# First chunk of a chunked delta-rule kernel: block products without doubles, and weight loads held behind the second inverse

## The chip, the cores and the metric

The kernel runs on one core of a Trainium2 chip. The metric is the device time of one execution in microseconds; of several runs the median is given. A core has five engines that run their own instruction queues side by side and wait for each other through semaphores: PE (matrix products, with PEld for the loading of its stationary operand), DVE (vector), ACT (scalar and activation), POOL (GpSimd) and SP (here only a queue that issues DMA transfers). Matrix products land in PSUM, eight banks of 2 KB on each of 128 partitions; DVE and ACT bring them from there to SBUF.

## The reference

Two stages. The first is a delta rule over 768 tokens for 4 batches of 8 heads, each with a 48x48 state; the second is a feed-forward layer over the 3072 tokens of width 384 that come out.

```python
for t in range(S):                                  # q, k, v: (4, 8, 768, 48)
    kt, vt, bt = (k_n[:, :, t], v[:, :, t], beta[:, :, t, None])   # k_n: k over its norm
    y[:, :, t] = np.einsum('bhd,bhde->bhe', q[:, :, t], state)
    v_old = np.einsum('bhde,bhd->bhe', state, kt)
    state = state + bt[:, :, :, None] * np.einsum('bhd,bhe->bhde', kt, vt - v_old)
...
x = y.transpose(0, 2, 1, 3).reshape(3072, 384)
h = x @ w_in                                        # 384 x 2048, 64-bit in memory
g = np.maximum(h, 0.0) + alpha * np.minimum(h, 0.0)
return g @ w_out                                    # 2048 x 384, 64-bit in memory
```

## The kernel before

**Tiling.** The delta rule is done in 12 chunks of 64 tokens (`C = 64`). Inside a chunk the recurrence becomes a triangular system with one 64x64 matrix per head and batch. A step is one chunk of two of the four batches: `steps` has 24 of them, and steps 0 and 1 are the first chunk. A tile of a step has 128 partitions, 64 for each of its two batches, and 8 heads beside each other. `half(t)` is one batch's 64 partitions, `a` is a head's parity and `g` its number among the four of that parity (`G = 4`).

**The triangular system.** For the first four steps (`NJ = 4`) only diagonal blocks of 16x16 (`LB = 16`) are inverted, by elimination on DVE (`eliminate_small`), with everything turned so that a partition holds one matrix. The results are turned back in four pieces twice: first into `turned`, then into `inverse` (`back`, stream transposes at L567; `PIECES = 4`). `off_products` multiplies the block inverses with what lies off the diagonal (`mid`), which gives `diag` and, with the two halves of the partitions exchanged, `away`. Three substitutions with these (`substitute` L732 on PE, `substituted` L738 to L754 on DVE) then do what the remaining blocks ask for, `solve` (L910) multiplies with the inverses that `place_inverse` (L759) has laid out, and `outputs` (L923) makes the chunk's output, whose masked factor `a_t` comes from `mask` (L1623).

For odd heads (`a = 1`) substitutions 0 and 2 of steps 0 and 1 read `away`, and substitution 1 reads the upper half of the heads of `diag` with the halves exchanged in its output.

**What is a double here.** In `off_products`, for each of the two steps, PE makes the product of every head for both halves into its own half (L687: 16 matmuls); for the four odd heads it makes the same product once more into the other half (L689: 8 matmuls), so that `away` can be copied from PSUM. One ACT copy per step takes `diag` out (L690, 128x384) and one DVE copy takes `away` (L693, 128x192). Each float32 matmul shows as two records in the profile.

**Order of the work.** The schedule is manual: each engine does its instructions in the order in which the program issues them, and semaphores that follow from the data keep them correct. Generators (`inverted`, `conv_in`, `first_in`) are advanced by hand between other work. `weave` and `alongside` mix the first feed-forward products (L1088) with the second pair of steps (`second_pair`). PSUM is given out in turn: `ps_big` rotates three tiles of two banks, so a product waits until the tile's reader of three turns ago is done.

**Weights.** `w_in` and `w_out` have 64-bit elements. The `weights` helper loads each piece as raw words into a stage (512 KB for a piece of `w_in`), ACT does two passes over it (`begin`, L262 and L263), and DVE two more (`finish`, L272 and L277), after which the stage is free for a later piece. `w_in` has 12 pieces; six stages lie in the space of `w_out`, two in `space_out`. `fetch_in(n)` issues loads up to piece n, `begin_in(n)` ACT's passes, and `convert(n)` advances the generator `conv_in`, which itself calls `begin` for up to `ahead[0]` or one piece ahead. The first feed-forward products need pieces 0 to 2 for the first 512 columns, 3 to 5 for the next, and so on.

**Loads.** All loads but three of the first keys go through SP's queue, in order: first keys, beta, v and q of steps 0 and 1 (96 KB for each half), six weight pieces, two more once beta's place is free, keys of steps 4 to 6, the second copy of keys of step 1, v of 2, q of 2 and 3. A load that must wait for its place holds all that is behind it on SP.

**Filling PE.** `busy` issues wide matmuls whose results nobody reads, in the time in which DVE eliminates (L1606).

Of the kernel before, what the change touches and what calls it, by code (L numbers as in the profile page):

```python
# [25 lines left out]
FP32 = mybir.dt.float32  # L26
# [6 lines left out]
C = 64  # L33
HB = 32
# [10 lines left out]
def kernel(  # L45
# [623 lines left out]
    def off_products(both):  # L669

        x = [act[:, FP - 4 + i].rearrange("p f i -> p (f i)") for i in both]
        x = [y.rearrange("p (h c) -> p h c", h=H) for y in x]
        for i in both:
            own = turned[0][:, i * H : i * H + H]
            nc.scalar.mul(x[i][:, :, 0:HB], own, which[:, 0:1])
            nc.vector.tensor_scalar_mul(x[i][:, :, HB:C], own, which[:, 1:2])
        n = C - LB
        own, other = [ps_big(), None], ps_big()
        own[1] = ps_big()
        for i in both:  # L680
            p = own[i][:, 0, 0 : H * n].rearrange("p (b i) -> p b i", b=H)
            q = (other[:, 0] if i == 0 else own[1][:, 1])[:, 0 : G * n]
            q = q.rearrange("p (b i) -> p b i", b=G)
            for b in range(H):
                for t in range(2):
                    w, y = x[i][half(t), b], mid[i][half(t), b, LB:C]
                    nc.tensor.matmul(p[half(t), b], w, y)  # L687
                    if b >= G:
                        nc.tensor.matmul(q[half(1 - t), b - G], w, y)  # L689
            nc.scalar.copy(diag[i][:, :, LB:C], p)  # L690
            other_.append(q)
        return [
            lambda i=i: nc.vector.tensor_copy(out=away[i][:, :, LB:C], in_=other_[i])  # L693
            for i in both
        ]

    other_ = []
# [912 lines left out]

    def queries():
# [17 lines left out]

    def first_chunk(mask, inverted, convert):  # L1630
# [3 lines left out]
        aways = off_products(both)  # L1634
        for _ in range(PIECES - 1):
            next(inverted)
        aways[0]()
        next(inverted)
        assert next(inverted, None) is None
        aways[1]()  # L1640
        place_inverse(0)
# [3 lines left out]
        for k in range(3):  # L1645
            for i in both:
                p = substitute(i, now_at[i], k)
                if k == 0:
                    now_at[i] = work.tile([128, 2, G, D], FP32, name="r")
                substituted(i, now_at[i], p, k)  # L1650
                if i == 0 and k < 2:
                    now(flipped(NJ + k, ps_one()))
                if (k, i) == (1, 0):
                    place_inverse(1)
                if (k, i) == (0, 1):
                    place(0, (3,))
                    for j in (3, 2):
                        off_blocks(j, by_pool=True)
                if (k, i) == (1, 1):
                    place(1, (3,))  # L1660
                    begin_in(6)
                if i == 0 and k > 0:
                    mask(0, k - 1)
        for i in both:
            squared(NJ + i)
# [4 lines left out]
        now(weighted)  # L1670
        for a in range(2):
            mask(1, a)
        now(keys)
        now(solve(1))
# [3 lines left out]
        load_early(NJ + NKE)  # L1678
# [33 lines left out]
    n_in = FT * DM // n  # L1712
    stages = [space[:, i * n : (i + 1) * n] for i in range(n_in)]
    spare_words = space_out.rearrange("p s e -> p (s e)")
    stages += [spare_words[:, i * n : (i + 1) * n] for i in range(2)]
    ids = [*range(n_in + 2), 0, 2, 1, 3]
# [31 lines left out]
    fetch_in(n_in)  # L1748
# [61 lines left out]
    fetch_in(n_in + 2)  # L1810
# [9 lines left out]
    load_v(2)  # L1820
    for i in range(2):
        flips(N, i)
    for i in range(2):
        load_q(i + 2)
# [9 lines left out]
    busy(BUSY - 3.5, mid[1], p)  # L1834
    for _ in range(6):
        busy(0.25, mid[1], p)
    begin_in(5)
# [302 lines left out]
```

## Time and profile before

| what | value |
|---|---|
| median of 3 runs | 631.5 us (630.01, 631.5, 636.12) |
| profiled execution, its own time | 632.44 us |
| its span, first to last instruction | 630.7 us |
| PE busy in the span | 617.4 us (98%), 9116 matmul records |
| PEld busy | 545.5 us (86%) |
| DVE busy | 504.0 us (80%) |
| ACT busy | 312.4 us (50%) |
| POOL busy | 99.9 us (16%) |
| mean granted PE clock | 0.997 |
| DMA in the span | 39.26 MB, mean 62 GB/s; 17.98 MB of it in the first 100 us |

A line of the timeline names the start in us, the length, engine, line and operation, what it writes and reads, shapes, the number of instructions merged and, in brackets, the idle time before it with its cause; "issue" is a wait for which the profile shows no cause. Matmuls overlap and their ends are modelled. In the table of stretches each engine has its busy time in the stretch, and the last three columns are the granted PE clock, the share of the 16 DMA engines' time and the rate. The queue q8 carries instructions.

### The profile page before, as it was taken

What the parts mean: (1) busy time and instruction counts of PE and PEld (TensorE: products, weight loads), DVE (VectorE), ACT (ScalarE), POOL (GpSimd) and SP (SyncE); (2) the same over time, 40 slices, a digit from 0 to 9 for tenths busy, and PEclk for the clock granted to TensorE, in tenths of its full rate; (3) what the DMA queues carried; (4) which work ended last, traced back from release to release, by engine and by line L of the source; (5) the groups of instructions that cost most, each with busy time, mean ns of one, the idle gap of its engine ahead of it and who ended that gap; (6) DMA issues with size and microseconds to landing.
All of it is one profiled execution on the core that took longest, in us unless ns stands there. A gap on an engine that the chain in (4) does not pass through costs nothing.

```text
span 630.7 us, 21675 instructions
## 1 busy us (share of the span) xinstructions
PE 617.4 (98%) x9116; PEld 545.5 (86%) x9116; DVE 504.0 (80%) x1223; ACT 312.4 (50%) x836; POOL 99.9 (16%) x218
## 2 busy tenths in 40 slices
PE   6989999999999999999999999999999999999997
PEld 5678788566789989989989989989999999999997
DVE  5978999979989988968978868878979579386383
ACT  6878566255544256446345446335356366352230
POOL 7032221010001000000000000000053062061350
PEclk9989999999999999999999999999999999999999
DMA  7958845212252241241341121211220300100100
GB/s 117 301 120 193 242 87 161 41 38 51 44 85 44 56 73 27 54 74 30 51 76 30 39 40 27 53 26 27 46 51 13 62 15 11 30 3 1 26 1 25
DMA packets 145968, 39.26 MB, mean 62 GB/s; under 512 B 139040, under 2 KB 142256, under 8 KB 145872
## 3 DMA queue, kind: packets, MB, share of 16 engines
q1 hardware_dynamic: 144000, 37.40, 29.0%
q8 instruction: 71, 1.16, 0.7%
q10 hardware_dynamic: 1872, 0.49, 0.4%
q14 instruction: 25, 0.20, 0.1%
HBM read 33.14 MB, written 4.72 MB: 60 GB/s over the span
## 4 chain that ended last, share of the span: by engine, by line
PE 87%; DVE 5%; ACT 3%; DMA 2%; issue 1%; SPq 1%; ACTq 0%; DVEq 0%
PE p_ffn L1088 16%; PE p_ffn L1152 10%; PE p_more L1088 8%; PE p_more L1422 8%; PE p_more L1152 8%; PE p_ffn L1131 5%; PE p_more L1338 5%; PE p_ffn L1328 3%; PE p_ffn L1422 3%; PE p_ffn L1333 3%; PE p_pair L885 2%; PE p_pair L923 2%; PE p_pair L809 2%; PE p_pair L910 2%; PE p_pair L502 2%; PE p_pair L867 2%
## 5 line engine op out<-in xcount | busy, mean ns | idle before, releaser
L1088 PE MATMUL p_ffn<-xt,w_in 128*128 128x256 f32 x528 | 123.2, 384 | 0.1
L1088 PEld LDWEIGHTS p_ffn<-xt,w_in 128*128 128x128 f32 x528 | 97.6, 190 | 14.1 <-issue 0.4
L979 ACT COPY xt<-z 32x96 f32<-32x96 f32 x240 | 64.5, 269 | 49.4 <-DVE z L966 46.3
L1088 PE MATMUL p_more<-xt,w_in 128*128 128x256 f32 x240 | 55.7, 382 | 0.0
L1362 POOL TENSOR_TENSOR k_t<-k_t 128x128 f32<-128x128 f32 (+1 forms) x48 | 28.3, 591 | 166.3 <-ACT k_t L1357 163.8
L600 DVE TENSOR_TENSOR block<-block,prod 128x30 f32<-128x30 f32 (+9 forms) x150 | 50.0, 333 | 5.1
L1088 PEld LDWEIGHTS p_more<-xt,w_in 128*128 128x128 f32 x240 | 44.9, 190 | 6.3
L594 DVE TENSOR_TENSOR prod<-block 128x30 f32<-128x30 f32 (+9 forms) x150 | 48.6, 324 | 1.3
L419 POOL TENSOR_TENSOR beta_t<-beta_t,rec 128x8 f32<-128x8 f32 x24 | 6.9, 288 | 231.8 <-DVE rec L413 228.0
L1100 DVE SCALAR_TENSOR_TENSOR act<-act,al_t,p_ffn 128x256 f32<-128x256 f32 x72 | 31.0, 471 | 14.5 <-ACT act L1098 14.4
L826 ACT COPY inv<-p_pair 32x256 f32<-32x256 f32 x30 | 10.9, 363 | 59.2 <-DVE u L914 35.5
L1098 ACT ACTIVATE act<-p_ffn 128x512 f32<-128x512 f32 x36 | 21.4, 594 | 22.7 <-PE p_ffn L1088 22.4
L1362 POOL TENSOR_TENSOR block<-block 128x128 f32<-128x128 f32 (+1 forms) x48 | 27.7, 577 | 12.6 <-ACT block L1357 10.1
L1328 PE MATMUL p_ffn<-xt,w_in 128*128 128x256 f32 x96 | 29.3, 387 | 0.0
L1152 PE MATMUL p_ffn<-w_out,act 128*128 128x192 f32 x160 | 27.7, 327 | 0.0
L914 DVE TENSOR_TENSOR u<-p_pair,wgt 128x384 f32<-128x384 f32 x24 | 13.2, 554 | 16.8 <-PE p_pair L910 9.9
L1152 PEld LDWEIGHTS p_ffn<-w_out,act 128*128 128x128 f32 x160 | 26.2, 190 | 0.3
L1100 DVE SCALAR_TENSOR_TENSOR act<-act,al_t,p_more 128x256 f32<-128x256 f32 x40 | 17.3, 474 | 10.9 <-ACT act L1098 10.7
L895 DVE TENSOR_TENSOR r<-v_raw,p_pair 64x192 f32<-64x192 f32 (+1 forms) x66 | 23.2, 352 | 2.1 <-PE p_pair L885 1.0
L1152 PE MATMUL p_more<-w_out,act 128*128 128x192 f32 x128 | 22.3, 326 | 0.0
L1357 ACT COPY k_t<-p_more 128x512 f32<-128x512 f32 x16 | 9.4, 587 | 25.5 <-PE p_more L1338 18.9
L1422 PE MATMUL p_more<-w_out,act 128*128 128x192 f32 x128 | 21.6, 327 | 0.0
(285 smaller groups left out, 1486.5 us busy)
## 6 DMA issues: line engine op xcount, KB each, us to landing
w_out<-in_moe_w_in_dram SPq DMA_DIRECT2D x10, 512.0 KB, 5.6
v_raw<-in_v_dram SPq DMA_DIRECT2D x48, 96.0 KB, 2.9
kl<-in_k_dram SPq DMA_DIRECT2D x96, 48.0 KB, 2.4
out_dram<-o_sb SPq DMA_DIRECT2D x90, 48.0 KB, 1.6
space_out<-in_moe_w_out_dram SPq DMA_DIRECT2D x11, 384.0 KB, 4.0
ke_last<-in_k_dram SPq DMA_DIRECT2D x25, 96.0 KB, 3.5
qp<-in_q_dram SPq DMA_DIRECT2D x64, 32.0 KB, 2.2
w_out<-in_moe_w_out_dram SPq DMA_DIRECT2D x5, 384.0 KB, 5.3
```

Source lines behind the costliest of these rows:

```text
L594: nc.vector.tensor_tensor(out=prod, in0=r[:, 0:j, j : j + 1].to_broadcast([128, j, n]), in1=r[:, j : j + 1, j + 1 : HB].to_broadcast([128, ...
L600: nc.vector.tensor_tensor(out=r[:, 0:j, j + 1 : HB], in0=r[:, 0:j, j + 1 : HB], in1=prod, op=ALU.add)
L895: nc.vector.tensor_tensor(out=r[to, a], in0=v_in[to, a], in1=p[own, a, :, 0:D], op=ALU.subtract)
L979: nc.scalar.copy(to[quad(r), u, bp, t], z[quad(2 * t + u), r])
L1088: nc.tensor.matmul(p_h[:, i], w_in[:, t, (f + i) * 128 : (f + i + 1) * 128], xt[:, t], start=(t == 0), stop=(t == KT - 1),)
L1100: nc.vector.scalar_tensor_tensor(out=g[:, i], in0=g[:, i], scalar=al_t[:, f + i : f + i + 1], in1=p_h[:, i], op0=ALU.mult, op1=ALU.add,)
L1131: nc.tensor.matmul(p_o[u], gs[f // 2][:, f % 2, u * 128 : (u + 1) * 128], w_out[:, f], start=(f == 0), stop=(f == FT - 1),)
L1152: nc.tensor.matmul(p, x(i), w(i), start=(i == 0), stop=(i == FP - 1))
L1328: nc.tensor.matmul(p[:, f * 256 : f * 256 + 256], w(2, f), xt[:, 2], start=True, stop=False)
L1338: nc.tensor.matmul(q[:, j], a, b, start=True, stop=True)
L1362: nc.gpsimd.tensor_tensor(out=dst, in0=a, in1=b, op=ALU.add)
L1422: nc.tensor.matmul(p, x(i), w(i), start=(i == 0), stop=(i == FP - 1))
```

## The change

In `off_products` the second products of the odd heads are gone. Odd heads are multiplied once, into the exchanged half; ACT copies the even heads to `diag` and the odd ones to `away`, and POOL copies `away`, halves exchanged, to the upper heads of `diag`. DVE copies nothing there. `spread` is new and adds 16 matmuls of 32x32 on the four quarters, in a bank that nobody reads; `busy` has half a matmul less.

Four weight pieces are fetched ahead (`LOADED`) and four are converted by ACT before the first chunk. `release`, called when the second inverse is placed, writes one element of the fifth piece's stage from that inverse, so that this piece's load, and all that SP has behind it, waits for it; behind it come q of step 2, keys of step 7, pieces 5 to 7, v of 2 and q of 3. The squares of keys of steps 4 and 5 are made earlier, the last piece of the inverse is turned after the first substitution, and the four masks are moved.

```diff
@@ off_products
-        n = C - LB
-        own, other = [ps_big(), None], ps_big()
-        own[1] = ps_big()
         for i in both:
-            p = own[i][:, 0, 0 : H * n].rearrange("p (b i) -> p b i", b=H)
-            q = (other[:, 0] if i == 0 else own[1][:, 1])[:, 0 : G * n]
-            q = q.rearrange("p (b i) -> p b i", b=G)
-            for b in range(H):
-                for t in range(2):
-                    w, y = x[i][half(t), b], mid[i][half(t), b, LB:C]
-                    nc.tensor.matmul(p[half(t), b], w, y)
-                    if b >= G:
-                        nc.tensor.matmul(q[half(1 - t), b - G], w, y)
-            nc.scalar.copy(diag[i][:, :, LB:C], p)
-            other_.append(q)
-        return [
-            lambda i=i: nc.vector.tensor_copy(out=away[i][:, :, LB:C], in_=other_[i])
-            for i in both
-        ]
-
-    other_ = []
+            p = region(None, G * (C - LB), g=G)
+            for g, a, t in quarters():
+                b = a * G + g
+                nc.tensor.matmul(
+                    p[half(t ^ a), a, g], x[i][half(t), b], mid[i][half(t), b, LB:C]
+                )
+            nc.scalar.copy(diag[i][:, 0:G, LB:C], p[:, 0])
+            nc.scalar.copy(away[i][:, :, LB:C], p[:, 1])
+            for t in range(2):
+                nc.gpsimd.tensor_copy(
+                    out=diag[i][half(t), G:, LB:C], in_=away[i][half(1 - t), :, LB:C]
+                )
@@ new
+    def spread(n, by, p):
+        for i in range(n):
+            rows = quad(i % 4)
+            nc.tensor.matmul(p[rows, 0:HB], ident[rows, rows], by[rows, 0, 0:HB])
+    def release():
+        nc.scalar.copy(held_back, inv[1][0:1, 0, 0:1])
+        fetch_in(LOADED + 1)
+        load_q(2)
+        load_early(NJ + NKE)
+        fetch_in(n_in + 2)
+        load_v(2)
+        load_q(3)
@@ first_chunk
-        aways = off_products(both)
+        off_products(both)
         for _ in range(PIECES - 1):
             next(inverted)
-        aways[0]()
-        next(inverted)
-        assert next(inverted, None) is None
-        aways[1]()
-        place_inverse(0)
...
                 substituted(i, now_at[i], p, k)
+                if (k, i) == (0, 0):
+                    squared(NJ)
                 if i == 0 and k < 2:
                     now(flipped(NJ + k, ps_one()))
+                if (k, i) == (0, 0):
+                    squared(NJ + 1)
+                    next(inverted)
+                    assert next(inverted, None) is None
+                    place_inverse(0)
                 if (k, i) == (1, 0):
                     place_inverse(1)
+                    release()
...
                 if (k, i) == (1, 1):
                     place(1, (3,))
-                    begin_in(6)
-                if i == 0 and k > 0:
-                    mask(0, k - 1)
-        for i in both:
-            squared(NJ + i)
+                if (k, i) == (2, 0):
+                    mask(0, 0)
...
         weighted = solve(0)
         keys = flipped(NJ + 2, ps_one())
         now(weighted)
+        mask(0, 1)
+        now(keys)
+        now(solve(1))
         for a in range(2):
             mask(1, a)
-        now(keys)
-        now(solve(1))
         convert(6)
         for i in both:
             now(outputs(i))
-        load_early(NJ + NKE)
         fetch_in(n_in + 4)
@@ body
+    LOADED = 4
+    held_back = stages[LOADED][0:1, 0:1].bitcast(FP32)
-    fetch_in(n_in)
+    fetch_in(LOADED)
...
-    fetch_in(n_in + 2)
...
-    load_v(2)
...
-    for i in range(2):
-        load_q(i + 2)
...
-    busy(BUSY - 3.5, mid[1], p)
+    spread(16, mid[1], [x for x in big if x is not turned_beta][0][:, 1])
+    busy(BUSY - 4, mid[1], p)
...
-    begin_in(5)
+    begin_in(4)
```

## The prediction

> **What bounds the kernel now.** The page first: PE is busy for 617.4 of 630.7 us, and its clock row reads 9 in every slice but one near the start. The change touches only work up to about 50 us, so the question is whether time won there reaches the long PE-bound rest. I then cut the start into stretches: us, busy time of PE, PEld, DVE, ACT and POOL, granted clock, DMA share, GB/s.
>
> ```profile
> 23.24:26.65 3.41, 3.41 (x9) 1.50 (x8) 2.93 (x13) 3.35 (x6) 0.00 (x0) 1.00 1.01 393
> 26.65:30.07 3.42, 2.75 (x57) 2.50 (x57) 3.38 (x9) 2.90 (x6) 0.00 (x0) 1.00 1.24 260
> 30.07:33.48 3.41, 3.41 (x170) 3.12 (x162) 2.56 (x7) 2.50 (x7) 1.84 (x3) 1.00 0.69 109
> 33.48:36.89 3.41, 1.64 (x65) 1.31 (x60) 1.13 (x5) 2.69 (x8) 2.97 (x6) 1.00 0.54 98
> 36.89:40.30 3.41, 3.41 (x94) 3.14 (x86) 2.80 (x7) 1.47 (x3) 0.00 (x0) 0.50 0.62 115
> 40.30:43.71 3.41, 2.92 (x108) 2.25 (x106) 2.89 (x7) 2.00 (x4) 0.00 (x0) 1.00 0.38 68
> ```
>
> There is one hole. In 33.48 to 36.89 PE works 1.64 us only, and in the next stretch it is granted half its clock. The PE timeline (start, length, instructions, idle before and its cause) shows the hole in the middle of the fourth substitution, between two like matmuls of one loop:
>
> ```profile
> 34.10 0.55 PE L732 MATMUL p_pair<-r,diag 64*64 64x48 f32 x21
> 36.41 0.39 PE L732 MATMUL p_pair<-r,diag 64*64 64x48 f32 x12 [1.77 <-issue]
> ```
>
> No engine and no data transfer is the cause given. I looked at the instruction queue: the page has 71 packets of 1.16 MB on q8, 16 KB each, and in the narrow view of the DMA one of them runs in 34 to 35 us, just before PE goes on. The one before runs at 23. At 18 to 30 us the DMA share stands at 0.95 to 1.45: eight weight pieces of 512 KB, then keys. So I read the hole as a late instruction block behind a full DMA, in the densest stretch of small matmuls, and the half clock as its echo.
>
> Last, what follows the first chunk, on ACT and DVE:
>
> ```profile
> 28.14 0.68 ACT L263 ACTIVATE w_out<-w_out 128x512 f32<-128x512 f32 x1
> 28.72 0.89 ACT L675 ACTIVATE act<-turned,which 128x256 f32<-128x256 f32 x2
> ...
> 48.03 0.60 ACT L1098 ACTIVATE act<-p_ffn 128x512 f32<-128x512 f32 x1 [1.17 <-PE p_ffn L1088]
> 48.90 0.48 ACT L707 COPY diag<-p_pair 128x384 f32<-128x384 f32 x1 [0.27 <-PE p_pair L704]
> 49.86 0.59 ACT L456 COPY k_t<-p_pair 112x512 f32<-112x512 f32 x1 [0.48 <-PE p_pair L430]
> ...
> 54.94 0.59 ACT L1098 ACTIVATE act<-p_ffn 128x512 f32<-128x512 f32 x1
> ```
>
> ```profile
> 55.56 0.87 DVE L1100 SCALAR_TENSOR_TENSOR act<-act,al_t,p_ffn 128x256 f32<-128x256 f32 x2 [2.04 <-ACT act L1098]
> ```
>
> ACT has 1.92 us of idle time in 46.86 to 49.86 and none from there to 55.5; DVE then waits 2.04 us for it and runs without a break to 63.9. The chain of waits agrees: ACT from 50.36, DVE from 55.56 to 74.3, then PE. So the second pair hangs on ACT, and a gain in the first chunk passes on only as far as ACT lets it.
>
> **The change, part by part.** I follow the chunk from the last turned transpose (28.41) to the second output product (L923, second group, 41.94).
>
> Start: ACT does four conversions before L675, not five (0.68 + 0.59 saved), so L675 waits only for the transpose and starts at 28.45 instead of 28.72.
>
> Products: 96 matmul records take 29.26 to 31.12. Now there are 64, each kind on all four quarters as in L732, which does 64 in 1.08 (32.50 to 33.58). The first substitution no longer waits for the second tile's products, but for two ACT copies of 128x192 (0.31 each by L742): 29.53 end of the first 32, some 0.2 until seen, copies to 30.37, start at 30.42 against 31.16. The two DVE copies (L693, 0.35) leave; the second of them held DVE until 32.28. The first sum on DVE starts at 31.0 (before 32.21). The last transpose piece (0.55 apart) now lies behind it, so the second sum starts at 32.1, not 33.18. **Gain 1.1.** POOL's two copies per tile (L709: 1.10 for two) run 30.4 to 32.6 and are needed by the third and fourth substitution at about 32.1 and 33.2: about 0.6 of cover each; without it each us late costs one. POOL's own `off_blocks` shifts by 1 us to end at 37.7, wanted at L704 (47.93 before).
>
> The hole: quiet DMA from about 27, since SP has four pieces fewer ahead of the keys. **Gain 1.77**, bounds 0 and 1.77. But a block must still come. From its packet's start at 34.06 to 36.41 are 2.35 us; packets elsewhere start 0.3 to 1.2 after the last block is used up (36.41 to 37.59 is one), so about 2.7 to 3.5 in all, while PE in the new schedule uses a block in about 2.8 to 3.2. I book 0.6 back for two smaller holes; bounds 0 and 1.8.
>
> The half clock: PE's 73 L732 records from 36.41 take 2.13 against 1.24 at the earlier rate, L910 0.96 against 0.54, L430 0.98 against 0.60, 1.7 together; DVE's sums lie between, so I take **1.0**, bounds 0 and 1.7. The trace ties it to the hole, as the stretch after the only half-empty one. The Trainium skill (TensorE: Matmul & The Clock Gate, Part 1) lets the clock fall only after a whole idle window of about 3.4 us; here 1.77 us idle was enough, so the measurement decides. By the page's rule the half clock would not hang on the hole and this gain would be 0.
>
> ACT order up to there: four copies 1.24, two squares 0.82, `k_t` 0.57, `place_inverse(0)` 0.91, `place` 0.40, `k_t`, `place_inverse(1)`, the tiny copy of `release` (0.20 by the 1x1 of L293; 0.1 to 0.4). Laid end to end from 29.75, the second `k_t` copy is out at 34.35, when the sixth substitution wants its bank (34.5), and the second inverse at 35.2, wanted at 36.2. Tight but covered; up to 0.3 late. Masks: the same four of 0.33 to 0.42, two of them now after the second `u`, right before the product that needs them; 0 to 0.7, in my schedule already. `spread` is 32 small matmuls (by L704, 64 in 0.88, about 0.45) for half a wide one (0.43), in front of a PE wait of 0.68 for L675: 0.
>
> Sum to L923: 1.1 + 1.77 + 1.0 - 0.6 = 3.3 us earlier.
>
> After it: pieces 4 and 5 are converted later. Program order puts them on ACT after the two L993 copies and ahead of pieces 6, 7 and the first L1098. That is two pairs of 1.27, 2.55 us, into a stretch with 1.92 of idle time: **0.65 back**. DVE has 2.04 of idle at 55.56 and adds nothing.
>
> Loads: SP waits from about 27 to 35.5 on the tiny ACT copy. Behind it stand piece 4, q of step 2, the keys of step 7, pieces 5 to 7, v of 2 and q of 3: 12 issues of 0.5 to 0.64, done at about 42.8, when pieces 8 and 9 wait for freed space anyway (42.88 before). Bytes: four pieces at 1.3 each (0.4 MB per us at 18 to 27) and four small loads at 1.1, about 10 us of DMA, done at about 46. Piece 5, issued at 39, lands at about 42 and ACT wants it at 42.1; 6 and 7 follow at 1.3, ACT's own pace. Keys and q of step 2 are read at 48.74 and 49.23 (45.4 shifted), v at 56.69. Cost 0 with hardly 0.5 us to spare for pieces 5 to 7; bounds 0 and, at the 11.7 us to landing that the two `space_out` pieces took under a full queue, 7.
>
> Net gain 3.3 - 0.65 = 2.65, after which PE-bound work repeats as before. The profiled execution took 632.44, 0.94 above the median of 631.5 (630.01 to 636.12): 632.44 becomes 629.8, and the median **628.9**.
>
> **Rivals.**
> A, all of it: blocks come in time and ACT catches up, since DVE had 2 us of room behind it. 1.1 + 1.77 + 1.0 and up to 0.7 more of the half clock: 3.9 to 4.6, so 627.2. For it: PE is hardly ever idle after 42; against: ACT without a gap from 49.86.
>
> B, the hole stays: the block is late because PE simply uses 256 instructions in 3.3 us there (31.1 to 34.4), not because of other transfers; moving it moves the hole too. For it: the small matmuls keep their density; against: the page's 71 blocks show one such hole in 630 us, right after the fullest DMA stretch. Gain 1.1 less 0.65, with the clock at half again: 631.0. The Trainium skill (Runtime: NRT & Kernel Launch, Instruction fetch mechanics) has blocks of 16 KiB fetched while the last one runs, with the cost mostly hidden. Block size agrees (1.16 MB over 71), "hidden" does not (1.77 us); by that rule the hole is something else and stays as in B.
>
> C, slower: the held pieces are late. One mechanism: ACT takes its queue in order, so piece 5 waiting for its transfer holds pieces 6, 7, L1098 and the copies of the second pair. Against before, ACT has 3.3 us less 0.65 in hand, so it decides from the point where these pieces land over 2.65 us later than I have them. At 11.7 us from issue at 40.3, piece 7 lands at 52.0 and ACT is 7 us behind my plan: 628.9 + 7 = 635.9. Against: those 11.7 had six pieces ahead of them at 1.0 share; pieces 8 and 9 took 4.6.
>
> **How the numbers follow.** Forecast 0.48 (627.8 to 630.2), A 0.20, B 0.20, C 0.12. Of C half lies under 633, of A a quarter under 626. The range 626.0 to 633.0 holds some 0.85 of it, and bounds of the terms (half clock 0 to 1.7, new holes 0 to 1.8) stay inside. Within 1%, what a measurement of this kernel can tell from no change, is 625.2 to 637.8: nearly all of the forecast, A, B and most of C. Faster by more: 0.07; slower by more: 0.07; same 0.86.
>
> **What would show it.** Right: no PE idle of over 1 us by "issue" in 29 to 42 and a clock of 1.00 in 36 to 41; the first L732 at about 30.4; the second L923 group at 38 to 39; SP issuing nothing from 27 to 35; ACT unbroken from the L993 copies to the second L1098, that one at 52 to 52.5, and DVE at L1100 at about 53. Wrong: a stall of PE by "issue" near 34 to 40 (B); ACT L262 waiting for DMA w_out or space_out at 41 to 47 (C); the second L1098 at 51 (A).

## The result: 0.47% slower

| | kernel before | changed kernel |
|---|---|---|
| median | 631.69 us (629.89 to 636.12, 21 executions) | 634.83 us (632.85 to 640.34, 21 executions) |
| profiled execution, its own time | 632.44 us | 634.09 us |
| its span | 630.7 us | 632.4 us |
| PE busy, matmul records | 617.4 us, 9116 | 618.5 us, 9114 |

The ratio is 1.0047, 95% interval 1.0029 to 1.0064: 3.1 us lost, where 2.65 us of gain were forecast. From the products on, line numbers are 8 smaller in the changed kernel (L732 is L724, L923 is L915, L1098 is L1090, L1100 is L1092).

**The profile after.** The stretches of the start, with the columns as before (engines in the order PE, PEld, DVE, ACT, POOL, then clock, DMA share, GB/s):

```profile
30.07:33.48 3.41, 3.41 (x140) 2.95 (x143) 2.44 (x6) 2.79 (x9) 3.07 (x7) 1.00 0.02 5
33.48:36.89 3.41, 3.20 (x142) 2.75 (x138) 2.77 (x7) 2.47 (x8) 2.90 (x6) 1.00 0.24 50
36.89:40.30 3.41, 2.61 (x88) 2.02 (x80) 3.04 (x7) 1.43 (x4) 0.00 (x0) 1.00 1.13 241
40.30:43.71 3.41, 3.41 (x74) 2.76 (x75) 3.31 (x8) 1.86 (x3) 0.00 (x0) 1.00 0.93 300
43.71:47.12 3.41, 3.41 (x81) 2.88 (x80) 3.16 (x7) 2.62 (x4) 0.00 (x0) 1.00 1.07 247
47.12:50.50 3.38, 2.24 (x73) 1.61 (x72) 1.65 (x4) 2.97 (x6) 0.59 (x2) 1.00 0.93 286
```

The last two of them in the kernel before:

```profile
43.71:47.12 3.41, 3.41 (x74) 2.79 (x74) 3.31 (x8) 3.00 (x5) 0.00 (x0) 1.00 0.70 202
47.12:50.50 3.38, 3.38 (x81) 2.85 (x80) 3.35 (x8) 1.72 (x4) 0.95 (x2) 1.00 0.84 202
```

The half-empty stretch and the half clock are gone. The DMA share is 0.02 where it was 0.69, and then about 1 for four stretches, where it was 0.62, 0.38, 0.70 and 0.84: the bytes have moved. PE is now short of work in the last of these (2.24 us busy, 3.38 before). Its timeline has the second output product and the wait behind it:

```profile
38.23 0.91 PE L915 MATMUL p_pair<-u,a_t 64*64 64x48 f32 x32 [0.70 <-DVE a_t L1621]
...
49.78 0.65 PE L430 MATMUL p_pair<-ident,qp 128*112 128x128 f32 x4 [1.14 <-ACT diag L699]
```

The product starts 3.71 us earlier than in the trace before (41.94). What comes then is seen on ACT:

```profile
43.95 0.68 ACT L262 ACTIVATE w_in<-w_out 128x512 uint32<-128x512 uint32 x1 [1.74 <-DMA w_out<-in_moe_w_in_dram]
...
47.50 0.69 ACT L262 ACTIVATE w_in<-space_out 128x512 uint32<-128x512 uint32 x1 [0.86 <-DMA space_out<-in_moe_w_in_dram]
...
48.78 0.58 ACT L1090 ACTIVATE act<-p_ffn 128x512 f32<-128x512 f32 x1
...
54.71 0.59 ACT L1090 ACTIVATE act<-p_ffn 128x512 f32<-128x512 f32 x1
...
70.62 0.57 ACT L262 ACTIVATE w_out<-space_out 128x384 uint32<-128x384 uint32 x1 [2.99 <-DMA space_out<-in_moe_w_out_dram]
...
75.90 0.55 ACT L262 ACTIVATE w_out<-w_out 128x384 uint32<-128x384 uint32 x1 [2.29 <-DMA w_out<-in_moe_w_out_dram]
```

Two held pieces of `w_in` come 1.74 and 0.86 us late. The first L1090 is at 48.78, later than before (48.03), the second at 54.71, as before (54.94): 3.7 us of lead are nearly used up on ACT. The first pieces of `w_out` are late as well. The kernel before waits for them too, but for less:

```profile
71.57 0.56 ACT L262 ACTIVATE w_out<-space_out 128x384 uint32<-128x384 uint32 x1 [2.18 <-DMA space_out<-in_moe_w_out_dram]
73.70 0.57 ACT L262 ACTIVATE w_out<-w_out 128x384 uint32<-128x384 uint32 x1 [0.96 <-DMA w_out<-in_moe_w_out_dram]
```

In the chain of work that ended last, these waits are in the changed kernel alone. Its chain passes there through the second `w_out` piece, where the chain of the kernel before runs on DVE from 55.56 to 74.65 (but for one ACT copy at 63.97):

```profile
64.85 5.75 DMA space_out<-in_moe_w_out_dram
70.62 0.57 ACT w_out L262
```

SP's timeline says why the pieces are late:

```profile
35.03 0.33 SPq L246 DMA_DIRECT2D w_out<-in_moe_w_in_dram  x1
...
38.17 0.80 SPq L246 DMA_DIRECT2D w_out<-in_moe_w_in_dram  x1
...
43.69 3.60 SPq L246 DMA_DIRECT2D w_out<-in_moe_w_in_dram  x2
...
57.74 3.33 SPq L169 DMA_DIRECT2D ke_last<-in_k_dram  x2
61.19 0.55 SPq L246 DMA_DIRECT2D space_out<-in_moe_w_out_dram  x1
```

It issues nothing from 28 to 35.03; the first `w_out` piece goes out at 61.19, 3.1 us later than before:

```profile
58.11 1.60 SPq L246 DMA_DIRECT2D space_out<-in_moe_w_out_dram  x1
```

For the whole course I counted PE's records from the end in two traces and took the difference in start of the same record, in us against the profiled execution before (minus is earlier; the times are those of the trace before):

```
                         34     42     60     80    300    625
before, profiled again  0.30  -1.25  -1.25  -0.73  -0.87  -0.87
changed kernel         -1.24  -3.54  -1.41   1.40   1.46   1.45
no_hold                 0.22  -0.29  -0.25   0.20   1.00   0.99
hold_alone             -0.26  -0.93   0.67   2.88   3.04   3.03
thin_held_pieces       -1.29  -2.84  -2.80  -1.10  -0.89  -0.91
hold_two_pieces        -1.27  -3.11  -2.23  -2.25  -2.30  -2.32
products_alone         -0.50  -2.63  -1.99  -2.05   3.13   3.12
products_and_spread    -0.42  -3.42  -3.44  -3.43  -3.37  -3.38
changed_without_spread -1.09  -3.62  -0.47   2.37   6.19   6.17
```

In the changed kernel 3.5 us are won by 42 us; 2.1 are lost by 60 and another 2.8 by 80, and then nothing changes for 550 us. Each column is one execution: that of no_hold is the longest of its 12 (634.17 us, with a median of 631.23), those of hold_two_pieces and products_and_spread the shortest of theirs.

### The profile page after: what moved, and what is told of

It is laid out like the page before. It is cut to its first block, busy times and chain, and to the rows that moved or that the text cites. A ratio compares the mean times of both kernels' runs of the same rounds, so it can differ in the third digit from the quotient of the medians.

```text
span 632.4 us, 21679 instructions
## 1 busy us (share of the span) xinstructions
PE 618.5 (98%) x9114; PEld 544.7 (86%) x9114; DVE 503.3 (80%) x1221; ACT 312.4 (49%) x839; POOL 100.6 (16%) x222
## 4 chain that ended last, share of the span: by engine, by line
PE 87%; DVE 6%; DMA 3%; ACT 1%; issue 1%; POOL 0%; SPq 0%; ACTq 0%; DVEq 0%; POOLq 0%
PE p_ffn L1080 16%; PE p_ffn L1144 10%; PE p_more L1080 8%; PE p_more L1414 8%; PE p_more L1144 8%; PE p_ffn L1123 5%; PE p_more L1330 5%; PE p_ffn L1320 3%; PE p_ffn L1414 3%; PE p_ffn L1325 3%; PE p_pair L877 2%; PE p_pair L801 2%; PE p_pair L915 2%; PE p_pair L502 2%; DMA qp<-in_q_dram 2%; PE p_pair L859 2%
## 5 line engine op out<-in xcount | busy, mean ns | idle before, releaser
L1092 DVE SCALAR_TENSOR_TENSOR act<-act,al_t,p_ffn 128x256 f32<-128x256 f32 x72 | 31.1, 473 | 17.9 <-ACT act L1090 17.9
L1090 ACT ACTIVATE act<-p_ffn 128x512 f32<-128x512 f32 x36 | 21.4, 595 | 20.5 <-PE p_ffn L1080 20.3
L1092 DVE SCALAR_TENSOR_TENSOR act<-act,al_t,p_more 128x256 f32<-128x256 f32 x40 | 17.3, 474 | 10.9 <-ACT act L1090 10.8
L1144 PE MATMUL p_more<-w_out,act 128*128 128x192 f32 x128 | 22.3, 326 | 0.0
L877 PE MATMUL p_pair<-beside,k_t 48*64 48x112 f32 x704 | 21.4, 259 | 0.4 <-ACT beside L458 0.2
```

The source lines that it names most:

```text
L877: nc.tensor.matmul(p[half(t ^ a), a, g], k_t[n][dims(a), g, half(t)], beside[bp][dims(a), t, g])
L1092: nc.vector.scalar_tensor_tensor(out=g[:, i], in0=g[:, i], scalar=al_t[:, f + i : f + i + 1], in1=p_h[:, i], op0=ALU.mult, op1=ALU.add,)
L1144: nc.tensor.matmul(p, x(i), w(i), start=(i == 0), stop=(i == FP - 1))
```

## The experiments

All ratios are against runs of the kernel before on the same chip.

| kernel | median us | ratio | 95% interval |
|---|---|---|---|
| no_hold | 631.23 | 1.0007 | 0.9989 to 1.0025 |
| no_hold_six_early | 632.50 | 1.0022 | 1.0002 to 1.0041 |
| hold_alone | 634.68 | 1.0053 | 1.0037 to 1.0069 |
| weights_first | 635.78 | 1.0070 | 1.0044 to 1.0097 |
| keys_first | 633.43 | 1.0042 | 1.0026 to 1.0057 |
| release_at_products | 634.38 | 1.0051 | 1.0033 to 1.0070 |
| thin_held_pieces | 631.87 | 1.0020 | 1.0002 to 1.0037 |
| hold_two_pieces | 630.96 | 1.0002 | 0.9982 to 1.0021 |
| hold_small_loads | 632.17 | 1.0010 | 0.9993 to 1.0027 |
| more_spread | 637.65 | one time | |
| before_again | 630.95 | 0.9987 | 0.9969 to 1.0004 |
| products_alone | 636.34 | 1.0082 | 1.0065 to 1.0099 |
| products_and_spread | 631.24 | 1.0015 | 1.0000 to 1.0029 |
| changed_without_spread | 638.51 | 1.0123 | 1.0108 to 1.0138 |
| hold_two_in_phase | 631.28 | 1.0014 | 0.9998 to 1.0030 |

### Is it the hold?

**no_hold**, **no_hold_six_early** and **hold_alone** take the change apart at the loads.

In no_hold the changed kernel issues the held loads again where the kernel before does; no_hold_six_early converts two pieces earlier on top of that:

```diff
@@ first_chunk
-                    release()
...
+        load_early(NJ + NKE)
         fetch_in(n_in + 4)
@@ body
-    fetch_in(LOADED)
+    fetch_in(n_in)
...
+    fetch_in(n_in + 2)
     cross(0)
...
+    load_v(2)
...
+        load_q(i + 2)
@@ no_hold_six_early also
-    begin_in(4)
+    begin_in(5)
...
+                    begin_in(6)
```

hold_alone is the kernel before with the reverse of these lines, `release` behind `place_inverse(1)`, and the squares of the keys ahead of it, since a held load overwrites their keys.

> The changed kernel with every load where it was before (eight weight pieces ahead, no wait of SP on the second inverse); products, squares, masks and the four early conversions stay changed. Theory (the hold gives the gain back through late loads): ACT waits for no weight piece between 41 and 48 us, and the kernel is faster than the changed one by 2 us or more, about 631 us. Whether PE's hole by 'issue' and the half clock come back says if they hang on the full DMA: if so the second L915 group stands at 40 to 41 us, if not at 38.2 as in the changed kernel. Rival (the two conversions moved behind the chunk cost it): still about 634.

> As no_hold, but ACT also converts five pieces before the chunk and the sixth in it, as before the change. Theory: 0.65 us faster than no_hold at most, since ACT had 1.9 us idle there. Rival (the moved conversions cost): 2 us or more faster than no_hold.

> The kernel before with the hold alone: four pieces ahead and converted, the later loads behind the second inverse in the changed kernel's order; products with doubles, masks as before. Squares of steps 4 and 5 stand a little earlier, since the held keys overwrite their source. If the hole comes from full DMA: no PE idle by 'issue' and clock 1.00 in 33 to 40, second L923 group at 39 to 39.5 instead of 41.9, and then the same waits of ACT, so 634 to 635.5. If it comes from PE's own pace: the hole stays, 636 or more.

Without the hold the change costs nothing that can be told (1.0007); the hold alone, put into the kernel before, costs as much as the whole change (1.0053). Converting two more pieces early, where 0.65 us of gain at most was expected, brings nothing (1.0022), so the 0.65 us that I booked for late conversions is not the loss.

But the hole of PE does not follow the DMA as I had it. The list of PE's waits of no_hold (line, total us, times, longest):

```profile
PE p_pair L430 <- DMA ke_pair<-in_k_dram: 1.2, 1, 1.2
PE p_pair L724 <- issue: 1.1, 1, 1.1
PE p_pair L902 <- issue: 0.7, 1, 0.7
```

and the stretches and PE's timeline of hold_alone:

```profile
30.07:33.48 3.41, 3.41 (x148) 3.06 (x145) 2.74 (x7) 2.90 (x8) 2.22 (x4) 1.00 0.03 7
33.48:36.89 3.41, 2.28 (x92) 1.89 (x93) 1.78 (x6) 2.41 (x8) 2.57 (x5) 1.00 0.14 25
```

```profile
35.45 0.39 PE L732 MATMUL p_pair<-r,diag 64*64 64x48 f32 x12 [1.06 <-issue]
39.73 0.45 PE L910 MATMUL p_pair<-r,inv 64*64 64x48 f32 x16 [1.03 <-issue]
```

With DMA shares of 0.03 and 0.14 there is still a hole of 1.06 us, and one of 1.03 after it. A quiet DMA alone does not remove them.

### When and in which order are the held loads released?

weights_first has the four pieces ahead of the small loads, release_at_products waits for `away` of the second tile (about 30 us) in place of the second inverse, and keys_first does not wait at all: four pieces, then the keys, then the other four. In the last two only the keys of step 7 still go out when the second inverse is placed.

```diff
@@ weights_first, release
-        fetch_in(LOADED + 1)
+        fetch_in(n_in + 2)
         load_q(2)
         load_early(NJ + NKE)
-        fetch_in(n_in + 2)
-        load_v(2)
         load_q(3)
+        load_v(2)
@@ release_at_products, behind off_products(both)
-        nc.scalar.copy(held_back, inv[1][0:1, 0, 0:1])
+        nc.scalar.copy(held_back, away[1][0:1, 0, LB : LB + 1])
@@ keys_first, behind the keys in body
+    fetch_in(n_in + 2)
+    load_v(2)
...
+        load_q(i + 2)
```

> The changed kernel with the held loads in another order: pieces 4 to 7 first, then q of step 2, keys of step 7, q of step 3, v of step 2. Theory: pieces 5 and 7 land 2 to 3 us earlier, ACT's waits of 1.74 and 0.86 us at 43 to 47 go, the second L1090 stands at about 52.3 instead of 54.7, and the kernel comes out 1.5 to 2.5 us faster than the changed one, 632 to 633, since the loads of w_out are as late as before. Rival (ACT's added work, not its waits): second L1090 within 0.7 us of 54.7 and still 634.

> The changed kernel with the hold released by the last copy of the block products (about 30 us) instead of the second inverse (35 us). Theory: DMA stands still for 3 us, not 8; ACT's waits for pieces shrink to under 1 us and the kernel stands between keys_first and the changed one, near 631.5. Rival (any hold puts the same loads behind each other): as the changed one, 634 to 635.

> The changed kernel without the wait: four weight pieces, then keys of steps 4 to 6 and the second copy of keys of step 1, then pieces 4 to 7, v of 2, q of 2 and 3 at once; keys of step 7 when the second inverse is placed. Theory (the idle DMA of 27 to 35 us is what is given back): no wait of ACT for a piece at 41 to 48, no wait of PE for keys of step 4 (1.2 us in no_hold), holes by 'issue' of 1 to 2 us together as in no_hold; 629 to 630.5 against about 631 before. Rival (the loads' order, not the pause, costs): still 633 or more.

All three miss the time of their theory; release_at_products and keys_first come out at that of their rivals. Sending the pieces first does not help. In weights_first ACT's waits for held pieces shrink from 1.74 and 0.86 to 0.48 and 0.58 us, but pieces 8 and 9 are issued at 49.00 instead of 43.69, and ACT waits there:

```profile
49.00 1.04 SPq L246 DMA_DIRECT2D w_out<-in_moe_w_in_dram  x2
...
54.01 0.67 ACT L262 ACTIVATE w_in<-w_out 128x512 uint32<-128x512 uint32 x1 [2.63 <-DMA w_out<-in_moe_w_in_dram]
```

An earlier or no release puts a full DMA into the first chunk, and in these two traces a hole is there, larger than before. The stretch and the timeline of PE in keys_first:

```profile
33.48:36.89 3.41, 0.27 (x19) 0.15 (x12) 0.00 (x0) 2.13 (x7) 3.09 (x7) 1.00 1.05 352
```

```profile
37.05 0.38 PE L724 MATMUL p_pair<-r,diag 64*64 64x48 f32 x11 [3.30 <-issue]
```

In release_at_products it is 2.0 us at L902 (share 1.04), with clocks of 0.86, 0.50 and 0.64 from 36.89 to 47.12. So the largest holes stand under a full DMA, and a quiet one leaves some of them. That the full DMA is what makes them large is likely but not shown: no run changes the DMA there and nothing else.

### How many bytes are late?

thin_held_pieces loads only an eighth of the words of pieces 4 to 7; the rest of these pieces is left out, and POOL sets its place to zero before. So it computes with a part of `w_in` missing. hold_two_pieces holds two pieces, which then go out first, and the small loads, hold_small_loads only q and v of steps 2 and 3 and the keys of step 7, with the keys of step 4 ahead of the last two pieces.

```diff
@@ thin_held_pieces, the load of a piece
+                if count == 12 and 4 <= i < 8:
+                    w, src = w[:, 0:128], src[:, 0:128]
@@ hold_two_pieces
-    LOADED = 4
+    LOADED = 6
...
-        fetch_in(LOADED + 1)
+        fetch_in(n_in + 2)
         load_q(2)
         load_early(NJ + NKE)
-        fetch_in(n_in + 2)
@@ hold_small_loads
-        nc.scalar.copy(held_back, inv[1][0:1, 0, 0:1])
-        fetch_in(LOADED + 1)
+        v_raw[2] = work.tile([128, H, D], FP32, name="v_raw", bufs=3)
+        nc.scalar.copy(v_raw[2][0:1, 0, 0:1], inv[1][0:1, 0, 0:1])
+        fetch(v, 2, v_raw[2])
...
-    fetch_in(LOADED)
+    fetch_in(n_in)
...
+    load_early(1 + NKE)
+    fetch_in(n_in + 2)
```

> The changed kernel with an eighth of the words of pieces 4 to 7 loaded (the rest of their stages is set to zero by POOL before); all waits and conversions stay. This leaves out part of w_in. Theory (time is given back because held bytes must pass in 36 to 53 us): ACT waits for no piece and for little of w_out, the lead of 3.5 us at 46 us stays to the end: 629 or less. Rival (ACT's two moved conversions and its order carry it): second L1090 still near 54 us and 633 or more.

> The changed kernel, but six weight pieces go out ahead instead of four; only pieces 6 and 7, q of steps 2 and 3, the keys of step 7 and v of step 2 are held for the second inverse. Theory (the later loss is the 2 MB of held weight, which ACT reaches before they land): 1 MB less is late, so the waits of ACT for pieces of w_in (1.74 and 0.86 in the changed kernel) go or fall below 0.5 in sum, the lead of 3.5 us at 42 us is mostly kept at 60 us (2 or more, against 1.4), the later w_out wait of 2.99 falls under 2, and the median is 1.5 to 3 us below that of the changed kernel, 0.997 to 1.002 of the kernel before. Rival (the hold itself costs, however little is behind it, or the hole in PE comes back with six pieces ahead): 1.003 or more, with the ACT waits at about their old size, or with a PE hole of over 1 us by issue in 31 to 42.

> The changed kernel with all eight weight pieces issued ahead as in the kernel before, and the keys of step 4 ahead of the last two; held for the second inverse are only v and q of steps 2 and 3 and the keys of step 7. Theory (the loss comes from late weight bytes alone, the hole from an instruction block under a full DMA): ACT waits for no piece of w_in, w_out pieces are issued within 1 us of before (58.1, 62.5, 65.3), but a PE hole of 0.7 to 2 us stands in 31 to 42, so the result is that of the changed kernel without the hold, 0.999 to 1.003. Rival (holding any loads costs the same as holding the weights): 1.004 or more with w_out waits of over 2 us on ACT.

With an eighth of the bytes the lead stays at 2.8 us from 42 to 60, with all of them it falls by 2.1: stage one of the loss is the bytes of the held pieces. But the median of thin_held_pieces is 631.87, where 629 or less was expected. Its trace loses 1.7 us between 60 and 80, and there PE stands still by "issue", without a late load as the cause (its lines are 3 further down than in the changed kernel):

```profile
59.40 0.38 PE L727 MATMUL p_pair<-r,diag 64*64 64x48 f32 x11 [0.69 <-issue]
70.47 0.34 PE L505 MATMUL p_pair<-k_t 48*64 48x64 f32 x7 [1.36 <-issue]
```

With two pieces held instead of four, no wait of ACT for `w_in` is left, and the second L1090 stands at 52.70 (52.60 in thin_held_pieces), close to the 52 to 52.5 of the forecast. What ACT still waits for in `w_out`:

```profile
ACT w_out L262 <- DMA space_out<-in_moe_w_out_dram: 3.4, 3, 1.8
ACT w_out L262 <- DVE v_raw L730: 0.6, 1, 0.6
ACT w_out L262 <- DMA w_out<-in_moe_w_out_dram: 0.3, 1, 0.3
```

The lead of 2.2 at 60 us reaches the end (2.3), and the ratio falls from 1.0047 to 1.0002; the two intervals do not overlap. So 1 MB more held, behind which everything on SP stands later, is what makes the change slower. The hoped-for gain over the kernel before does not come in any of them. hold_small_loads gives the ratio that was expected, but not the hole of 0.7 to 2 us: none is over 0.4 us in the chunk, at a share of 0.95 from 30.07 to 33.48. So a busy DMA does not always bring a hole.

### What is the hole?

In every trace these holes of PE by "issue" stand after records 960, 1216, 1472 and so on, matmuls, weight loads and PE's own semaphore instructions counted together: multiples of 256 apart, to one record. After holes of over 0.45 us PE goes on 1.2 to 1.8 us after the end of a 16 KB packet on q8 (once 0.9). more_spread adds 64 matmul records and as many weight loads (less four) to no_hold, ahead of the first chunk; before_again is the kernel before.

```diff
@@ more_spread, against no_hold
-    spread(16, mid[1], [x for x in big if x is not turned_beta][0][:, 1])
-    busy(BUSY - 4, mid[1], p)
+    spread(48, mid[1], [x for x in big if x is not turned_beta][0][:, 1])
+    busy(BUSY - 5, mid[1], p)
```

> no_hold with 32 more matmuls of spread (64 records, four records of busy fewer). If the hole is an instruction block that is late, holes stay at PE record 960 and 1216, now some 60 records earlier in the program (in the third or early fourth substitution and the sixth). If it belongs to a place of the program, they stay at the fourth substitution and the first solve, records 1020 and 1276.

> The kernel before, unchanged, profiled a second time. Theory (the forecast took its gains from one profiled execution, and the hole of 1.77 us and the half clock after it are not the same in every execution): the profiled execution shows other holes in PE at the same records of the instruction stream, of 0 to 2 us in sum, and the mean granted clock of the timed executions spreads from 0.995 to 1.000, with the longer executions at the lower clock. Rival (hole and half clock are in each execution): a hole of 1.7 to 1.8 us at 34 to 36.5 and a clock of 0.5 in the stretch after it again.

The holes keep their place in the stream and come some 60 matmul records earlier in the program: they belong to instruction blocks of 256. more_spread also has two new ones, of 1.19 and 1.30 us, at 342 and 369 us, far behind the edit. In before_again the holes have other sizes, 0.73 and 0.48 us, and no half clock follows:

```profile
35.67 0.39 PE L732 MATMUL p_pair<-r,diag 64*64 64x48 f32 x12 [0.73 <-issue]
39.40 0.45 PE L910 MATMUL p_pair<-r,inv 64*64 64x48 f32 x16 [0.48 <-issue]
```

Of the 113 executions of the kernel before that were timed beside these runs, 85 had a mean clock of 0.999 or more and a median of 630.5; 21 had 0.997 and a median of 632.25. The other seven, at 0.994 to 0.996, have a median of 631.2, so the clock alone does not give the time. One stretch of 3.41 us at half clock is 0.5 x 3.41 / 630 = 0.0027 of the clock, which fits the 0.997. The execution that was profiled before (0.997 and 632.44) is of the same kind as the 21. In the changed kernel 7 of 21 executions are at 0.997 or less, against 28 of these 113: its trace without a half clock does not show that half clocks have become rarer.

Then I took the products by themselves: products_alone is the kernel before with `off_products` as in the change's diff, and nothing else. Its result led to three more.

```diff
@@ products_and_spread, against products_alone
+    spread(16, mid[1], [x for x in big if x is not turned_beta][0][:, 1])
     busy(BUSY - 3.5, mid[1], p)
@@ changed_without_spread, against the changed kernel
-    spread(16, mid[1], [x for x in big if x is not turned_beta][0][:, 1])
@@ hold_two_in_phase, against hold_two_pieces
-    spread(16, mid[1], [x for x in big if x is not turned_beta][0][:, 1])
+    spread(17, mid[1], [x for x in big if x is not turned_beta][0][:, 1])
```

> The kernel before with the new block products alone: 64 matmul records instead of 96, two ACT copies of 128x192 and two POOL copies per step instead of one ACT copy of 128x384 and one DVE copy. All loads, conversions, squares, masks and the last piece of the inverse stay where the kernel before has them. Theory (the products save about 1 us as forecast, but the instruction block after record 960 comes no earlier because of that, so PE gives most of it back in front of it): the last turned transpose to the first substitution is 0.5 to 0.8 us shorter, a hole of 1 to 2.5 us by issue stands at record 960 of the stream, and the ratio is 0.998 to 1.001. Rival 1 (what is won at the products reaches the end in full): 0.9975 or less, 1.5 us or more. Rival 2 (the POOL copies come late for the third and fourth substitution and PE waits for POOL there): 1.001 or more, with idle time of PE at L724 put down to POOL.

> products_alone with the 16 small matmuls of spread put back in front of the wide ones: PE has 64 records fewer in the first chunk and 64 more before it, so that from the first substitution on every 256th record lies where the kernel before has it. Theory (the 5 us that products_alone loses at 242 and 271 us are instruction blocks that end inside a run of 64 tiny matmuls, because the stream is shifted by 64 records; spread is there to take the shift back): both holes are gone, PE has no idle time by issue of over 0.5 us after 80 us, and the ratio falls from 1.0082 to 0.996 to 1.000. Rival (the products themselves cost the 5 us, through POOL or the order of the pieces): it stays at 1.005 or more.

> The changed kernel without the 16 small matmuls of spread and with nothing in their place. Forecast as put on record: spread costs nothing and brings nothing, so taking it out changes nothing, 1.003 to 1.006 like the changed kernel. Theory of the instruction blocks: the stream after it is shifted by 64 records, holes by issue of 1.3 to 1.8 us stand near 243 and 269 us with a half clock after each, and the time is 4 to 6 us above the changed kernel, 1.011 to 1.015.

> hold_two_pieces with 17 matmuls in spread instead of 16, which makes up for the four records of the half wide matmul that the change takes out: every 256th record after the first chunk lies exactly where the kernel before has it. Theory (four records matter little, the tuned place is some 10 records wide): 0.998 to 1.001, not told apart from hold_two_pieces at 1.0002. Rival (the changed kernel sits at the edge of the tuned place, as the holes of 0.4 to 0.7 us at 182 us in two of its variants suggest): 0.5 to 1 us faster than hold_two_pieces, 0.997 to 0.999.

products_alone is 5 us slower, for a reason that none of its forecasts had, and not where it was changed: at 200 us its trace is 2 us ahead, at 300 it is 3.1 behind. Its timeline of PE there:

```profile
242.57 0.19 PE L801 MATMUL p_pair<-diag,right 32*32 32x32 f32 x1
244.33 0.18 PE L801 MATMUL p_pair<-diag,right 32*32 32x32 f32 x1 [1.57 <-issue]
...
245.56 6.99 PE L1144 MATMUL p_ffn<-w_out,act 128*128 128x192 f32 x32
...
272.83 0.21 PE L801 MATMUL p_pair<-inv,mid 32*32 32x32 f32 x1 [1.42 <-issue]
```

and its stretches (clock third from the end):

```profile
241.69:245.10 3.41, 1.84 (x100) 1.58 (x92) 2.03 (x5) 0.00 (x0) 0.47 (x2) 1.00 0.12 14
245.10:248.51 3.41, 3.41 (x13) 3.31 (x12) 1.38 (x5) 3.14 (x8) 0.00 (x0) 0.55 0.02 5
```

Two holes of 3.0 us together, in the middle of loops of tiny matmuls, the first at a DMA share of 0.12 (the second at 0.60, in 269.34 to 272.76); after the first the clock is half and the 32 wide matmuls behind it take 6.99 us. In the trace before the same ones take

```profile
245.69 5.36 PE L1152 MATMUL p_ffn<-w_out,act 128*128 128x192 f32 x32
```

so 1.63 more. 3.0 + 1.63 is most of the 5.1. The blocks, worked out from records and packets:

```
products_alone        first record   packet on q8       256th record   next record
records 7617 to 7872      240.89     241.62 to 242.86       242.57        244.33
before
records 7617 to 7872      240.24     235.96 to 237.16       244.22        244.22
```

Taking 32 matmuls out of the first chunk shifts every later block by 64 records. Now one block lies so that PE runs through it in 1.68 us (242.57 less 240.89), and the next was still on its way. Why the next packet had not come earlier, as the one in the trace before did, is not shown. With `spread` put back the holes are gone. The same stretch of products_and_spread:

```profile
241.69:245.10 3.41, 3.41 (x22) 3.33 (x21) 1.37 (x5) 2.73 (x7) 0.00 (x0) 1.00 0.00 0
```

and 1.0082 becomes 1.0015 (0.996 to 1.000 was expected). The changed kernel without `spread` has them too (1.0123, which is 0.76% or some 4.8 us over the changed kernel):

```profile
248.93 0.22 PE L801 MATMUL p_pair<-inv,mid 32*32 32x32 f32 x2 [1.83 <-issue]
...
275.89 0.25 PE L801 MATMUL p_pair<-diag,right 32*32 32x32 f32 x4 [1.56 <-issue]
```

The rival, that the products themselves cost it, falls; 1.0123 is what the theory of the blocks gave, though in this trace no half clock follows these two holes. `spread` keeps the later blocks where they were. Whether the four records that are still missing matter can't be told (hold_two_in_phase and hold_two_pieces have overlapping intervals).

## Why the prediction was wrong, point by point

- **Start and products, gain 1.1:** held in the changed kernel. At 34 us, just ahead of the hole of before, it is 1.24 us ahead, and DVE's first sum starts at 30.79 (31.0 forecast). The products alone give only 0.4 to 0.5 there; the rest then comes from what else is moved (a conversion, the last piece of the inverse, squares, masks).
- **The hole, gain 1.77, and the half clock, 1.0:** right as a forecast of this trace, which has no hole and a clock of 1.00; the second L915 at 38.23 (38 to 39 forecast), 3.7 us of lead for 3.3. As a gain over the median it was too large. Both were read off one execution, of the kind that has a clock of 0.997 (21 of 113) and takes 1.7 us more than the 85. It stands 1.9 us above the median of these (632.44 less 630.5); I took 0.94 off, so about 1.0 us of the gain was not there to be had. That the trace after has no hole is in part luck: holes and half clocks differ from one execution to the next.
- **Two small holes, 0.6 back:** none of over 0.3 us in the first chunk.
- **Rival B,** that PE simply uses a block faster than the next comes: right as a mechanism, from hold_alone and products_alone. The full DMA, which I held against it, may add to it. That the page showed one such hole in 630 us was no evidence against B: the blocks of the kernel before happen to lie well, shifts by 64 and 124 records bring holes at 243, 271, 342 and 369 us, and `spread`, which I booked at 0, takes the first of these shifts back. The sum was right at 0, but what it covers has a price that I did not name: 0.67 to 0.76%, 4 to 5 us. I also read that packets start 0.3 to 1.2 us after the last block is used up; in the same trace it is -0.9 to 4.1.
- **Loads, "Cost 0 with hardly 0.5 us to spare for pieces 5 to 7; bounds 0 and 7":** this is the step that failed. Piece 5 was to land at 42 and to be wanted at 42.1; it was issued at 38.17 and wanted at 42.2, and ACT got it at 43.95, 1.74 us late, and piece 7 another 0.86 late. I had the bytes done at about 46; the share is still 0.93 from 47.12 to 50.50. The term that was mis-sized is the rate. I took 0.4 MB per us from 18 to 27 us of the kernel before, where 109 of 971 packets are under 512 bytes (395 GB/s at a share of 1.01). From 36.89 to 50.50 of the changed kernel 4304 of 4997 are, as the pieces run there among small loads, and the same full DMA (1.02) moves 268 GB/s: its 3.65 MB take 13.6 us, not 9. The lead falls by 2.1 by 60 us, in the place of the 0.65 for late conversions.
- **What I had not followed at all** is the queue behind the held loads. Pieces 8 and 9 take SP until 47.3, all that follows on SP is later, the first `w_out` piece by 3.1 us, and another 2.8 us go between 60 and 80, where the chain of the changed kernel hangs on the second `w_out` piece. I had stopped at the second L1098. By the runs without, with half and with all of the hold (1.0007, 1.0002, 1.0047), holding four pieces costs 0.40 to 0.45%, 2.5 to 2.8 us of the median; by thin_held_pieces (1.0020) their bytes alone 0.27%. Each ratio has an interval of some 0.0018 to both sides.
- **Rival C** named the mechanism (ACT in order, held pieces late), with 635.9 at 12%. Its sign, ACT's L262 waiting for DMA at 41 to 47, is in the trace. Its sum is close to the time by luck: it has piece 7 at 52.0 (47.50 in the trace) and nothing of `w_out`, where more than half of the loss arises.

Still open: why the first chunk's own gain of 1.2 us does not show in the median even where nothing is held late. In those traces blocks are late at other places (hold_two_in_phase has holes by "issue" of 0.3 to 1.2 us before 37.91, 43.82, 60.52 and 78.56 us), and they differ between the two traces of the kernel before. What sets the time from the first use of a block to the start of the next packet (between -0.9 and 4.5 us in the first 60 us of all these traces) I could not find. None of the kernels beats the kernel before.

## What to carry to other kernels

A load that is moved behind a wait does not cost only its own lateness: follow the in-order queue behind it to the last thing that anyone waits for, and book a margin of 0.1 us as a loss. Take the rate of a transfer from a stretch with the same mix of packet sizes. Before a gap is booked as a gain, see whether it stands in most executions; the mean clock of each execution is a first sign of that. When matmuls are taken out of an unrolled kernel, look far behind the edit as well: the blocks of the instruction stream shift, and filler in an idle time can put them back.

## What the runs showed of the hardware

- **PE's instructions come in blocks of 256,** one packet of 16 KB each. In products_alone PE used one in 1.68 us; the next packet started 0.73 us after the block's first record, took 1.24, and PE went on 1.47 us after its end: 3.4 us in all. The Trainium skill (Runtime: NRT & Kernel Launch, Instruction fetch mechanics) has the 256 instructions and the 16 KiB, and these runs agree; it also says that the fetch is hidden by the rate at which instructions are issued, and two runs of tiny matmuls show otherwise by 1.57 and 1.42 us.
- **The clock falls after less than an idle window.** Stretches of 3.41 us in which PE was busy 1.64 and 1.84 us were followed by about half the clock; after one with 2.28 (hold_alone) it stayed at 1.00. So it did after 2.00 (keys_first, 31.75 to 35.16), 2.01 (hold_alone, 37.62 to 41.03) and 2.06 (products_alone, 269.34 to 272.75), and it fell after 1.39 to 1.78 in four other traces. Busy time does not settle it alone: in changed_without_spread the clock fell after 2.19 (12.16 to 15.57). The Trainium skill (TensorE: Matmul & The Clock Gate, Part 1) asks for a whole idle window of about 3.4 us; the measurement decides.
